# Linear attention and a gated MLP in one kernel: Tile orders the engines' queues by its detailed timing simulation instead of its simple one

## The chip, the cores and the metric

The kernel runs on one core of one Trainium2 chip. The time is the device time of one execution in microseconds (us), as the median over several runs. The core has five engines with a queue each: TensorE (PE, with its weight loads as PEld), VectorE (DVE), ScalarE (ACT), GpSimd (POOL) and SyncE (SP). SyncE's queue here issues nearly all transfers between the chip's memory and the core; ScalarE's queue issues the stores of the attention result and of the output.

## What is computed

Two stages follow one another. The first is attention with random features for 8 batches and 8 heads of 576 tokens with 64 channels, and 128 features; the second is a gated layer over the 4608 tokens of 512 channels with 1536 hidden columns.

```python
def phi(x):
    proj = np.einsum('bhsd,md->bhsm', x, omega)
    sq = np.sum(x * x, axis=-1, keepdims=True) / 2.0
    h = proj - sq
    h = h - np.max(h, axis=-1, keepdims=True)
    return np.exp(h) / np.sqrt(m)
q_p, k_p = (phi(q_s), phi(k_s))
kv = np.einsum('bhsm,bhsd->bhmd', k_p, v)
z = np.sum(k_p, axis=2)
num = np.einsum('bhsm,bhmd->bhsd', q_p, kv)
den = np.einsum('bhsm,bhm->bhs', q_p, z)[..., None] + 1e-06
attn = (num / den).astype(np.float32)

x = attn.transpose(0, 2, 1, 3).reshape(B * S, H * D)
gate = 1.0 / (1.0 + np.exp(-(x @ w_gate)))
val = x @ w_val
out = (gate * val @ w_out).astype(np.float32)
```

The weights arrive as 64-bit floats and are converted on the core.

## The kernel before

**How the numbers are kept.** A 32-bit operand of a large product is split in two parts: `split` (lines 68 to 71) writes a rounded high part with ScalarE (L70) and the remainder with VectorE or GpSimd (L71). Each product then takes three matmuls: low by high, high by low, high by high. `from_float64` (L74 to L97) turns a piece of the 64-bit weights into 32-bit floats with six VectorE instructions (L78, L81, L85, L89, L93, L95) and one addition on GpSimd (L96). The pieces are called `e` for the first eight column tiles and `c` for the 14 pieces after them; a `c` piece also gets four GpSimd subtractions (L173) and is stored to a scratch tensor `w32` in memory (L174).

**Attention** (L486 to L695). Tokens are taken two batches at a time, heads in pairs, by generators that yield between steps. `norms` loads tokens (`nat`, L492), squares them on ScalarE (L494) and sums them on VectorE (L496, L500). `projected` loads a transposed operand (`raw`, L512), splits it (`hi`, `lo`), multiplies it with omega (`pp`, L540 to L542), and takes maxima on VectorE (`mx` L545, `hm` L549). `keys` loads values (`v`, L564), takes exponentials on ScalarE (`kp`, L580), multiplies them with the values (`pkv`, L588) and copies the result (`kv`, L593). `queries` subtracts on VectorE (`sub` L606, `h` L608), transposes on TensorE (`pt`, L619), takes exponentials (`qp`, L621), multiplies with `kv` (`pn`, L631), divides on VectorE (`den` L636, `inv` L640, `x` L642), transposes back (`px`, L648), copies on ScalarE (`xs`, L654) and stores to a scratch tensor `xT` (L656). Up to six such generators are active at a time and take turns (`attention`, L674).

**The gated layer.** `first_pass` (L220) loads 512 tokens from `xT` (`load`, L217), splits them (`xe`), and for the first four hidden column tiles forms gate and value products (`gv`, L240), a tanh (L261) and a product on VectorE (L268), which is stored (`ye`, L273). Its steps are traced between attention steps, as soon as the attention result that they need has been traced. `second_pass` (L387) does the other hidden columns by a seven-product scheme for 2 x 2 blocks (`operands` L277, `gated` L326, matmuls `gw` at L344); units of weights come back from `w32` and are split (`unit`, L185). `last` (L436) loads the gated values (`yr`, L431 and L433), splits them, multiplies them with the output weights (`po`, L458), combines and stores the output.

**What sets the order in a queue.** The Python code traces instructions in one program order. When the context of Tile, the library that it is written in, closes, Tile plays the program through a simulated machine. On each engine it takes, among the instructions whose operands and buffers the simulated machine finds ready, the one that was traced first. The order in which they were taken is the order of that engine's queue on the chip, and the semaphores are set for it. Buffers of a tag (`bufs=`) are given out in the same play, so an instruction that needs a buffer waits there for its release. An instruction can be pinned behind the one traced before it on its engine:

```python
pin = tc.keep_in_program_order
...
pin(nc.scalar.activation(out=p1, in_=v0, func=AF.Copy))
```

Pinned are the second pass's matmuls, its elementwise work and its stores, the work of `operands`, and the loads of `gated_values`. Not pinned are attention, the conversions, `load`, the first pass, the first units, and in `last` everything but the loads. PSUM has eight banks: six of tag `at`, two of tag `gv`; `any_bank` takes them in turn.

## Time and profile before

| | |
|---|---|
| median of 3 runs | 1264.21 us |
| lowest and highest | 1254.57, 1267.41 us |
| the profiled execution, its own time | 1253.32 us |
| its span, first to last instruction | 1251.5 us |
| instructions | 23829 |
| chain that ended last, TensorE's share | 74% |
| moved by DMA | 219.41 MB, mean 175 GB/s |

The profiled execution's own time is its span and what lies around it. In the profile a group is named by its line and by the tiles that it writes and reads: `ppk` is the `pp` tile of keys, `ppq` that of queries, and so on. SPq and ACTq are the DMA queues of SyncE and ScalarE. "A <- B" in a table of waits means that A's engine stood idle until B was done. A TensorE that is busy is not at its peak, since matmuls are pipelined and their ends are modelled.

### The profile page before, as it was taken

The page shows a single profiled execution, that of the slowest core. Times are in us where ns is not written, and L with a number is a line of the kernel's source. Part 1 is how long each engine was busy: PE and PEld are TensorE (multiplying, and loading weights), DVE is VectorE, ACT ScalarE, POOL GpSimd, SP SyncE. Part 2 cuts the span into 40 slices and gives each one's busy share as a digit, 9 for nine tenths or more (in the row PEclk, how much of TensorE's full clock was granted, in tenths as well). Part 3 has the DMA queues.
Part 4 walks back from the last instruction along what each step waited for, and adds up shares of the span by engine and source line. Part 5 has one row for each costly group of instructions (what it writes and reads, how often), then busy time and mean ns, then how long its engine had stood idle before and what let it go on. Part 6 is the DMA issues. An engine that isn't in the chain of part 4 may idle for free.

```text
span 1251.5 us, 23829 instructions
## 1 busy us (share of the span) xinstructions
PE 1179.0 (94%) x8828; PEld 1115.9 (89%) x8828; DVE 857.7 (69%) x1799; ACT 531.4 (42%) x1160; POOL 543.9 (43%) x577
## 2 busy tenths in 40 slices
PE   6889879999998999999999999999998899999998
PEld 6789868888787988778999999999998899999998
DVE  4887797997978565542666656665658787777773
ACT  5545565565553645252423232332225343434331
POOL 2545255554766423032366666666665311111110
PEclk7687989999999999999999999999999999999999
DMA  7655767777674532172432333233337676666662
GB/s 254 218 183 178 244 228 256 262 249 257 210 255 172 180 97 84 45 247 98 173 122 90 123 123 125 106 134 123 123 117 257 198 229 198 202 187 189 191 195 93
DMA packets 102356, 219.41 MB, mean 175 GB/s; under 512 B 10848, under 2 KB 41824, under 8 KB 98144
## 3 DMA queue, kind: packets, MB, share of 16 engines
q1 hardware_dynamic: 85392, 198.94, 47.6%
q10 hardware_dynamic: 16848, 18.95, 4.3%
q8 instruction: 70, 1.15, 0.4%
q14 instruction: 46, 0.38, 0.1%
HBM read 141.82 MB, written 76.02 MB: 174 GB/s over the span
## 4 chain that ended last, share of the span: by engine, by line
PE 74%; DVE 11%; DMA 6%; issue 4%; POOL 3%; ACT 2%; SPq 1%; ACTq 0%; DVEq 0%; POOLq 0%
PE gw L344 27%; PE po L458 20%; PE gv L240 11%; PE pnq L631 4%; PE pkv L588 4%; PE ptq L619 2%; DMA natk<-kn 1%; DVE mxq L545 1%; DMA xT<-xsq 1%; PE ppk L540 1%; DVE hmq L549 1%; PE pxq L648 1%; PE ppk L541 1%; POOL xe L71 1%; PE ppk L542 1%
## 5 line engine op out<-in xcount | busy, mean ns | idle before, releaser
L344 PE MATMUL gw<-xl,u 128*128 128x256 f32 x3024 | 363.5, 283 | 3.6 <-DVE u L324 3.6
L344 PEld LDWEIGHTS gw<-xl,u 128*128 128x128 f32 x3024 | 362.5, 190 | 4.5 <-DVE u L324 4.4
L458 PE MATMUL po<-u,yh 128*128 128x256 f32 x1512 | 272.3, 283 | 0.0
L458 PEld LDWEIGHTS po<-u,yh 128*128 128x128 f32 x1512 | 234.9, 191 | 0.0
L458 PE MATMUL po<-u,yl 128*128 128x256 f32 x756 | 214.4, 284 | 3.5 <-DVE yl L71 3.5
L240 PE MATMUL gv<-xe,wh 128*128 128x512 f32 (+1 forms) x640 | 202.5, 389 | 5.2 <-POOL xe L71 5.0
L70 ACT ACTIVATE yh<-yr 128x896 fp32r<-128x896 f32 x108 | 100.1, 950 | 159.1 <-PE po L458 88.5
L458 PEld LDWEIGHTS po<-u,yl 128*128 128x128 f32 x756 | 144.5, 191 | 4.1 <-DVE yl L71 4.1
L240 PEld LDWEIGHTS gv<-xe,wh 128*128 128x128 f32 x640 | 116.3, 192 | 25.3 <-POOL xe L71 9.7
L71 POOL TENSOR_TENSOR yl<-yr,yh 128x896 fp32r<-128x896 f32 x17 | 38.0, 2238 | 215.5 <-PE po L458 126.8
L240 PE MATMUL gv<-xe,wl 128*128 128x512 f32 (+1 forms) x320 | 124.3, 390 | 5.2 <-ACT ge L261 3.0
L71 DVE TENSOR_TENSOR yl<-yr,yh 128x896 fp32r<-128x896 f32 x91 | 100.8, 1123 | 29.3 <-PE po L458 17.1
L324 DVE TENSOR_TENSOR u<-gw,p 128x256 f32<-128x256 f32 x144 | 60.7, 422 | 58.1 <-PE gw L344 49.8
L71 POOL TENSOR_TENSOR lok<-rawk,hik 128x256 fp32r<-128x256 f32 (+1 forms) x80 | 56.3, 722 | 95.9 <-ACT hik L70 92.3
L71 POOL TENSOR_TENSOR loq<-rawq,hiq 128x256 fp32r<-128x256 f32 (+1 forms) x80 | 59.9, 761 | 78.1 <-ACT hiq L70 78.0
L588 PE MATMUL pkv<-v,kpk 128*128 128x66 f32 x512 | 85.1, 292 | 9.1 <-ACT kpk L580 8.5
L588 PEld LDWEIGHTS pkv<-v,kpk 128*128 128x128 f32 x512 | 78.8, 214 | 16.4 <-ACT kpk L580 14.2
L449 DVE TENSOR_TENSOR yr<-yr 128x128 f32<-128x128 f32 x144 | 60.6, 455 | 40.9 <-DMA yr<-ye 40.5
L71 POOL TENSOR_TENSOR xe<-xr,xe 128x512 fp32r<-128x512 f32 (+1 forms) x40 | 49.9, 1264 | 87.3 <-ACT xe L70 85.9
L631 PEld LDWEIGHTS pnq<-kv,qpq 128*128 128x128 f32 (+1 forms) x640 | 70.8, 190 | 9.0 <-ACT qpq L621 5.1
L631 PE MATMUL pnq<-kv,qpq 128*128 128x66 f32 (+1 forms) x640 | 74.7, 273 | 3.6 <-ACT qpq L621 3.0
L580 ACT ACTIVATE kpk<-ppk,nb 128x128 f32<-128x128 f32 x256 | 69.6, 391 | 15.3 <-DVE nb L567 15.2
(108 smaller groups left out, 2159.5 us busy)
## 6 DMA issues: line engine op xcount, KB each, us to landing
yl<-yl SPq DMA_DIRECT2D x36, 896.0 KB, 3.8
yr<-yl SPq DMA_DIRECT2D x72, 448.0 KB, 3.8
xr<-xT SPq DMA_DIRECT2D x68, 256.0 KB, 4.4
c<-w SPq DMA_DIRECT2D x14, 1024.0 KB, 6.3
w<-c SPq DMA_DIRECT2D x14, 1024.0 KB, 4.5
v<-va SPq DMA_DIRECT2D x32, 330.0 KB, 4.0
natk<-kn SPq DMA_DIRECT2D x36, 256.0 KB, 4.7
natq<-qn SPq DMA_DIRECT2D x36, 256.0 KB, 3.9
```

The lines of the kernel that those rows point to most:

```text
L70: nc.scalar.activation(out=hi, in_=x, func=AF.Copy)
L71: (lo_engine or nc.vector).tensor_tensor(out=lo, in0=x, in1=hi.bitcast(F32), op=ALU.subtract)
L240: nc.tensor.matmul(gv, lhsT=u[:, s], rhs=v, start=(m == 0), stop=(m == 3 * KC - 1))
L324: return nc.vector.tensor_tensor(out=o, in0=a, in1=b, op=ALU.add)
L344: nc.tensor.matmul(o, lhsT=u[:, k, s], rhs=v[:, kc, :], start=(first and m == 0), stop=(m == 5), skip_group_check=not first,)
L449: nc.vector.tensor_tensor(out=raw[:, o], in0=raw[:, a], in1=raw[:, b], op=op)
L458: nc.tensor.matmul(o, lhsT=u[:, i, :], rhs=v[:, k, :], start=(j + m == 0 and n in (1, 6, 5, 4)), stop=(j == NPAIR - 1 and m == 2), skip_gr ...
L540: nc.tensor.matmul(o, lhsT=lo[:, c], rhs=omH, start=True, stop=False)
L580: nc.scalar.activation(out=kp[t][:, h, :], in_=pp[:, 2 * i + h, :], func=AF.Exp, bias=nb[:, t - t0, h : h + 1], scale=SCALE,)
L588: nc.tensor.matmul(pkv[:, h, :], lhsT=kp[b * MID + i][:, h, :], rhs=v[:, i, h, :], start=(i == 0), stop=(i == MID),)
L619: nc.tensor.transpose(out=pt[:, i, :], in_=h_sb[:, i, :], identity=id_sb)
L631: nc.tensor.matmul(pn[r, 2 * i + h, :], lhsT=qp[:, 2 * i + h, r], rhs=kvs[u, p, bb][:, h, :], start=True, stop=True,)
```

## The change

One argument of the context is set. The traced program is the same, instruction for instruction; the simulated machine that Tile plays it through is another one. The simple machine runs an engine's instructions one after another with a duration each. The detailed one models, for each engine, a sequencer and a queue of issued instructions of limited length apart from the engine itself, the travel of semaphore updates, transfers that share the DMA engines, and a TensorE clock that depends on its activity. The rule of choice (ready, then traced first) and the pins stay.

```diff
     out = nc.dram_tensor("out", (B * S, DM), F32, kind="ExternalOutput").ap()
-    with tile.TileContext(nc) as tc:
+    with tile.TileContext(nc, schedule_with_timeline_sim=True) as tc:
         attn_glu_kernel(tc, *args, out)
```

## Prediction

> **What bounds the kernel now.** I read the page's first two parts, then a table of stretches, then the waits of TensorE and of the SyncE DMA queue in the first 560 us, then two short pieces of timeline. The page first: busy time, share of the span, instructions; and the granted TensorE clock in 40 slices, in tenths.

> ```profile
> PE 1179.0 (94%) x8828; PEld 1115.9 (89%) x8828; DVE 857.7 (69%) x1799; ACT 531.4 (42%) x1160; POOL 543.9 (43%) x577
> PEclk7687989999999999999999999999999999999999
> ```

> TensorE is busy for 1179.0 of 1251.5 us, so at most 72.5 us of idle time can be won from it, and the clock is below full almost only in the first six slices (188 us). The stretches show where both losses lie (length, then busy us of PE, PEld, DVE, ACT, POOL; granted clock; DMA share; GB/s):

> ```profile
> 0.00:200.00 200.00, 162.07 (x1026) 150.88 (x1026) 148.58 (x325) 111.49 (x302) 89.83 (x99) 0.81 0.66 218
> 200.00:400.00 200.00, 184.88 (x1296) 162.15 (x1296) 176.86 (x380) 106.86 (x291) 121.76 (x125) 0.98 0.69 241
> 400.00:560.00 160.00, 152.47 (x1027) 133.05 (x1028) 93.46 (x240) 79.91 (x204) 46.76 (x56) 1.00 0.40 129
> 560.00:940.00 380.00, 379.65 (x3009) 371.42 (x3008) 216.37 (x453) 113.48 (x217) 223.69 (x261) 1.00 0.33 123
> 940.00:1000.00 60.00, 53.28 (x411) 52.05 (x410) 47.09 (x77) 25.74 (x34) 25.95 (x23) 0.94 0.70 228
> 1000.00:1251.50 251.50, 246.62 (x2067) 246.41 (x2065) 175.31 (x327) 93.94 (x113) 35.91 (x16) 1.00 0.60 185
> ```

> TensorE's idle time is 37.9 + 15.1 + 7.5 = 60.5 us before 560 (attention woven with the first GLU pass), and 0.4 + 6.7 + 4.9 = 12.0 us after it. So the first 560 us are bounded by chains between engines with TensorE close behind, and the rest by TensorE itself. In the first stage TensorE waits for these (in all, times, longest; the first four of fifteen rows, and the last):

> ```profile
> PE ptq L619 <- DVE hq L608: 13.4, 12, 2.6
> PE ppk L540 <- POOL lok L71: 9.6, 2, 8.1
> PE pkv L588 <- ACT kpk L580: 8.5, 9, 1.9
> PE gv L240 <- POOL xe L71: 5.0, 11, 1.6
> ...
> PE pnq L631 <- DVE xq L642: 0.6, 1, 0.6
> ```

> The fifteen rows sum to 59.1 us. One wait of 8.1 us is the start, before any operand has arrived, and no order removes it: 51.0 us are left. All of it is for elementwise results, none for a load directly.

> **Part 1: what the change does.** No operation is added or removed. Every tile, buffer count, transfer and matmul stays. What moves is the place of an instruction in its engine's queue, and which buffer of a tag it gets. Tile takes, on each engine, the earliest instruction of the program that its simulated machine finds ready; the change swaps the machine. So the cost of the edit is the difference between two orders, and nothing in this trace shows the second one. I bound it by stage.

> **Part 2: after 560 us, zero.** Matmuls and elementwise work of the second pass carry an explicit pin to the instruction traced before them on their engine, so they keep their order. The output stage (`last`) is not pinned, but its matmuls accumulate over six pairs in four banks, and its loads are pinned. TensorE's waits there, in two groups, are part of the 12.0 us idle. The gain is at most 12.0 us; the loss I bound by another turn of the transition at 940 to 1000, 6.7 us. I take 0: what covers the elementwise work is TensorE at 0.4 us idle in 380.

> **Part 3: the first 560 us, what order can win.** Nothing here is pinned. How far is the present order wrong for the chip? The clearest witness is SyncE's DMA queue, where a command that cannot start holds all loads behind it:

> ```profile
> SPq L273 <- DVE ye L268: 57.7, 13, 16.3
> SPq L174 <- POOL c L173: 52.2, 14, 5.9
> SPq L217 <- DMA xT<-xsq: 47.3, 12, 8.9
> SPq L512 <- POOL lok L71: 43.4, 23, 6.1
> SPq L564 <- PE pkv L588: 38.6, 12, 5.4
> SPq L512 <- POOL loq L71: 27.1, 18, 5.7
> SPq L564 <- PE pxq L648: 18.2, 4, 5.7
> SPq L273 <- DVE denq L636: 12.7, 1, 12.7
> ```

> Two kinds are mixed. The L273 and L174 rows are stores whose data did not exist yet, and L217 is a load of attention output whose store had not landed: 57.7 + 52.2 + 47.3 + 12.7 = 169.9 us in which the queue was ordered as if producers and transfers were faster than they are. The L512 and L564 rows are loads whose buffer was still read: 43.4 + 38.6 + 27.1 + 18.2 = 127.3 us, which a better order cannot give a buffer, only move out of others' way. The first kind is 169.9 / 297.2 = 57%. The compute queues err in the same manner; ACT, POOL and PE at 25 us:

> ```profile
> 25.61 0.28 ACT L593 ACTIVATE kv<-pkv 128x132 f32<-128x132 f32 x1 [2.95 <-PE pkv L588]
> 25.79 1.52 ACT L70 ACTIVATE hik<-rawk 128x256 fp32r<-128x256 f32 x5
> 26.27 4.07 POOL L71 TENSOR_TENSOR lok<-rawk,hik 128x256 fp32r<-128x256 f32 x6 [15.28 <-ACT hik L70]
> 27.05 0.58 PE L540 MATMUL ppk<-omH,lok 128*128 128x256 f32 x1 [1.48 <-POOL lok L71]
> ```

> ScalarE stood 2.95 us at a copy that waited for TensorE, with five splits of loaded keys queued behind it; TensorE then ran dry for 1.48 us for the splits. If 57% of the 51.0 us is such misordering, a machine that times things right wins at most 29 us. At the other end it wins nothing, because the later operand only takes the place of the earlier. With no row that favours either end I take the middle, 14 us.

> **Part 4: the clock.** A stall here is paid twice. DVE and TensorE around 176 us, and two stretches:

> ```profile
> 174.31 0.15 DVE L549 SCALAR_TENSOR_TENSOR hmq<-mxq,sqq 128x4 f32<-128x4 f32 x1
> 174.37 1.22 DVE L89 SCALAR_TENSOR_TENSOR c<-c 128x1024 uint32<-128x1024 uint32 x1
> 175.51 0.72 DVE L606 TENSOR_TENSOR subq<-sqq,hmq 128x4 f32<-128x4 f32 x1
> 176.26 0.69 DVE L496 TENSOR_REDUCE ssq<-x2q 128x8 f32<-128x512 f32 x1
> 176.86 0.68 DVE L608 SCALAR_TENSOR_TENSOR hq<-ppq,subq 128x512 f32<-128x512 f32 x1
> ```

> ```profile
> 177.69 1.09 PE L619 MATMUL ptq<-id_sb,hq 128*128 128x128 f32 x4 [2.59 <-DVE hq L608]
> ```

> ```profile
> 174.00:178.00 4.00, 1.41 (x12) 1.19 (x11) 3.96 (x7) 3.04 (x7) 1.41 (x2) 0.96 0.97 343
> 178.00:181.00 3.00, 3.00 (x16) 3.00 (x15) 2.57 (x4) 1.01 (x2) 0.35 (x1) 0.50 0.31 82
> ```

> After 2.59 us without a matmul the next 3 us run at 0.50. Over 0 to 200 the clock is 0.81 in 162.07 us of busy time: 162.07 x 0.19 = 31 us of lost speed as an upper end. If 14 of 51 us of stalls go, 27% of that would go with them, 8 us; at the other end none, since the dips hang on the few longest gaps. I take half, 4 us.

> [...]

> **The sum.** 0 + 14 + 4 = 18 us. The profiled execution took 1253.3 us (span 1251.5): 1235. It lies 0.9% under the median of the runs, 1264.2, which is what will be compared, so 1264.2 - 18 = 1246 us. At the good end 29 us of stalls and, with 57% of the stalls, 57% of 31 = 17.7 us of clock: 1264.2 - 46.7 = 1217.5.

> **Rivals.** *Nothing to gain (about 1264).* The waits are for buffers and for chains that have no slack, not for order. For it: the 127.3 us of buffer waits; DVE at 176.86 of 200 us in the second stretch, where any order keeps it full. [...] That the two machines give almost one order is the same case: 1264.

> *Slower (about 1290).* The same piece of timeline shows it. Between hmq and subq, 0.15 us each but for their waiting, stands a weight conversion of 1.22 us, and between subq and hq a reduction of 0.69: work that was ready filled a moment in which the chain was not. A machine with longer delays between dependent instructions finds the chain unready more often, and puts such fillers into more of the groups.

> ```profile
> L608 DVE SCALAR_TENSOR_TENSOR hq<-ppq,subq 128x512 f32<-128x512 f32 (+1 forms) x80 | 49.3, 628 | 0.2
> ```

> Now 12 of the 80 groups make TensorE wait, 13.4 us, 1.1 us each. With 24 more it is 27 us, 1264.2 + 27 = 1291. It decides against the change from about 30 more groups on if the 18 us are won elsewhere as well, and from 12 more on (13 us) if they are not. Against it: the present machine already lets fillers in, and after 400 us DVE has room (93.46 of 160).

> **How the numbers follow.** A measurement of this kernel can tell about 1% from no change, 12.6 us: under 1251.6 is faster, over 1276.8 slower. My forecast, faster through fewer misplaced commands, has 0.42, at 1246. No gain or a gain below 1% has 0.30. Slower by fillers has 0.28. The likeliest case's own range is 1217 to 1252; the range that should hold eight in ten goes from the middle of its better half, 1222, to the slower rival's price, 1290.

> **What would show it.** Part 3 is right if the L273, L174 and L217 waits of the SyncE queue fall well under 169.9 us in the first stage and TensorE's idle time before 560 us falls from 60.5 to about 46; if those waits fall and the idle time stays, the first rival holds. Part 4: the clock of the first 200 us rises from 0.81 to about 0.84. Part 2: TensorE's idle time from the start of the second pass to the end stays near 12 us. The slower rival shows as more than 12 waits of ptq for hq, each behind a conversion or reduction on DVE. The forecast is wrong if attention simply ends later because TensorE was given first-pass matmuls ahead of the short attention steps: then the stretch before 560 us is longer at equal idle time, and the dense matmuls after it are fewer.

## The result and the profile after

The changed kernel takes **1316.26 us** (median of 4 runs, 1311.83 to 1322.52) against 1259.91 us for the kernel before (4 runs beside it): a ratio of **1.0446, interval 1.0369 to 1.0524**. It is slower by 56 us; 1246 us was forecast. Times here and below are medians of all executions of a kernel, while ratios leave out slow ones, over 1.5% above the kernel's fastest: two of four of `q_group`, one of four of `t_elem`, one of ten of `t_all`.

First the page of the changed kernel: busy time, share of the span, instructions of each engine; then the granted clock in 40 slices.

```profile
PE 1191.3 (91%) x8828; PEld 1133.2 (87%) x8828; DVE 877.9 (67%) x1799; ACT 529.9 (40%) x1160; POOL 547.8 (42%) x577
PEclk7568878899999999989999999999999999999999
```

The numbers of instructions are those of before. The busy times have hardly moved, but TensorE's share fell from 94% to 91%: the same work, with more idle time in it. The chain that ended last says where it was lost. From the chain of the kernel before, in order of time (start, length, what), the start of the second pass:

```profile
611.74 329.96 PE gw L344 x2766
```

And from the chain of the changed kernel:

```profile
670.47 330.07 PE gw L344 x2766
```

The second pass starts 58.7 us later and takes as long as before: the spans, 1251.5 and 1310.0 us, differ by 58.5. So all of the loss is made before that point. The last copy of an attention result to be stored (`xs`, L654) starts at 528.6 us before and at 586.0 us after, 57.4 us later, so it is made while attention lasts. I cut the two kernels at those moments (length, then busy us of PE, PEld, DVE, ACT, POOL; granted clock; DMA share; GB/s). The kernel before:

```profile
0.00:528.60 528.60, 469.19 (x3220) 422.01 (x3221) 404.25 (x927) 282.35 (x774) 248.79 (x271) 0.92 0.59 199
528.60:1251.50 722.90, 709.79 (x5610) 693.94 (x5608) 453.41 (x872) 249.07 (x387) 295.10 (x306) 0.99 0.47 158
```

The changed kernel:

```profile
0.00:586.00 586.00, 481.02 (x3219) 438.68 (x3220) 420.65 (x927) 281.42 (x773) 251.00 (x271) 0.88 0.54 180
586.00:1310.00 724.00, 710.27 (x5610) 694.56 (x5609) 457.25 (x872) 248.48 (x387) 296.76 (x306) 0.99 0.46 158
```

The same numbers of instructions, to one, lie on each side of the cut, and the second rows are equal within 1.1 us in length. In the first rows TensorE's idle time goes from 528.6 - 469.2 = 59.4 to 586.0 - 481.0 = 105.0 us, 45.6 more, and its busy time grows by 11.8 us while the clock falls from 0.92 to 0.88. Idle time and longer busy time together are the 57.4 us.

What TensorE waits for in that stage, in the changed kernel (total us, times, longest):

```profile
PE ptq L619 <- DVE hq L608: 24.1, 14, 8.5
PE pkv L588 <- ACT kpk L580: 18.0, 10, 7.4
PE ptq L619 <- DVE hmq L549: 10.8, 3, 8.1
PE ppk L540 <- POOL lok L71: 8.5, 1, 8.5
PE pxq L648 <- DVE xq L642: 7.9, 8, 3.1
```

The waits for `hq` were 12 of 13.4 us in all and are 14 of 24.1: hardly more of them, but longer ones, up to 8.5 us. The longest is shown here in the timeline of TensorE and then of VectorE (start, length, engine, line, operation):

```profile
77.92 0.90 PE L619 MATMUL ptq<-id_sb,hq 128*128 128x128 f32 x3 [8.51 <-DVE hq L608]
```

```profile
73.30 0.15 DVE L549 SCALAR_TENSOR_TENSOR hmq<-mxq,sqq 128x4 f32<-128x4 f32 x1
73.37 0.67 DVE L496 TENSOR_REDUCE ssk<-x2k 128x8 f32<-128x512 f32 x1
73.97 1.21 DVE L89 SCALAR_TENSOR_TENSOR c<-c 128x1024 uint32<-128x1024 uint32 x1
75.10 0.15 DVE L606 TENSOR_TENSOR subq<-sqq,hmq 128x4 f32<-128x4 f32 x1
...
75.41 1.26 DVE L496 TENSOR_REDUCE ssk<-x2k 128x8 f32<-128x512 f32 x2
76.59 0.68 DVE L93 TENSOR_SCALAR c<-c 128x1024 uint32<-128x1024 uint32 x1
77.19 0.68 DVE L608 SCALAR_TENSOR_TENSOR hq<-ppq,subq 128x512 f32<-128x512 f32 x1
```

Between `hm` and `h` of a group of queries stand two conversion steps and three reductions of other work, 3.8 us, with TensorE dry. That the conversions are early here shows in their tiles (issue time min/median/max in ns, first and last start). Loads of `c` pieces in the kernel before:

```profile
L142 SPq DMA_DIRECT2D c<-w x14: 327/332/1262, 86.9 to 383.3; - x14
```

In the changed kernel:

```profile
L142 SPq DMA_DIRECT2D c<-w x14: 328/328/423, 59.5 to 251.7; - x14
```

VectorE has a wait that grew in the same stretch, too. In the kernel before and in the changed one (first 620 us):

```profile
DVE denq L636 <- PE pnq L631: 44.3, 38, 5.1
```

```profile
DVE denq L636 <- PE pnq L631: 68.4, 31, 8.0
```

Here VectorE's queue stands still for a short matmul of the attention, on average 1.2 us before and 2.2 us after. So there are two suspects, one on each side of the pair: work that fills VectorE's queue ahead of what TensorE needs, and work that fills TensorE's queue ahead of what VectorE needs. The last suspect shows in the order of TensorE's queue. Up to the last transpose back (`px`, L648), the first pass's matmuls (`gv`, L240) stand in runs of these lengths between attention matmuls:

```
                   gv matmuls   runs   mean length   matmuls in runs of 12 or more
before                 642       157       4.1               102
changed                642        75       8.6               418
```

A product `gv` is a group of 12 matmuls. The simple machine slips attention matmuls in between; the detailed one mostly lets a whole group go, or two (418 of 642 matmuls stand in runs of 12 or more).

### The profile page after: what moved, and what is told of

The parts are those of the page before. It is cut to its first block, busy times and chain, and to the rows that moved or that the text cites. A ratio compares the mean times of both kernels' runs of the same rounds, so it can differ in the third digit from the quotient of the medians.

```text
span 1310.0 us, 23809 instructions
## 1 busy us (share of the span) xinstructions
PE 1191.3 (91%) x8828; PEld 1133.2 (87%) x8828; DVE 877.9 (67%) x1799; ACT 529.9 (40%) x1160; POOL 547.8 (42%) x577
## 4 chain that ended last, share of the span: by engine, by line
PE 72%; DVE 14%; DMA 8%; ACT 2%; issue 2%; POOL 1%; SPq 1%; ACTq 0%; DVEq 0%; POOLq 0%
PE gw L344 26%; PE po L458 20%; PE gv L240 14%; PE pnq L631 3%; PE pkv L588 3%; DMA xT<-xsq 2%; PE ptq L619 2%; DVE mxq L545 2%; DMA c<-w 1%; DVE hq L608 1%; DMA e<-w 1%; DMA xr<-xT 1%; DVE hmq L549 1%; DVE ssk L496 1%; DMA natk<-kn 1%
## 5 line engine op out<-in xcount | busy, mean ns | idle before, releaser
L240 PE MATMUL gv<-xe,wh 128*128 128x512 f32 (+1 forms) x640 | 190.0, 384 | 2.7 <-POOL xe L71 2.7
L70 ACT ACTIVATE yh<-yr 128x896 fp32r<-128x896 f32 x108 | 99.4, 949 | 158.8 <-PE po L458 76.9
L240 PEld LDWEIGHTS gv<-xe,wh 128*128 128x128 f32 x640 | 119.1, 197 | 23.3 <-POOL xe L71 4.2
L240 PE MATMUL gv<-xe,wl 128*128 128x512 f32 (+1 forms) x320 | 122.1, 391 | 7.9 <-ACT xe L70 7.7
L71 POOL TENSOR_TENSOR yl<-yr,yh 128x896 fp32r<-128x896 f32 x17 | 37.2, 2186 | 218.4 <-ACT yh L70 194.8
L71 POOL TENSOR_TENSOR lok<-rawk,hik 128x256 fp32r<-128x256 f32 (+1 forms) x80 | 59.7, 760 | 135.6 <-ACT hik L70 123.1
L71 DVE TENSOR_TENSOR yl<-yr,yh 128x896 fp32r<-128x896 f32 x91 | 97.0, 1099 | 17.1 <-ACT yh L70 17.0
L588 PE MATMUL pkv<-v,kpk 128*128 128x66 f32 x512 | 84.9, 299 | 18.5 <-ACT kpk L580 18.0
L449 DVE TENSOR_TENSOR yr<-yr 128x128 f32<-128x128 f32 x144 | 65.8, 497 | 49.5 <-DMA yr<-ye 48.9
L588 PEld LDWEIGHTS pkv<-v,kpk 128*128 128x128 f32 x512 | 78.6, 219 | 22.5 <-ACT kpk L580 21.4
L71 POOL TENSOR_TENSOR loq<-rawq,hiq 128x256 fp32r<-128x256 f32 (+1 forms) x80 | 58.1, 737 | 88.7 <-ACT hiq L70 87.4
L619 PE MATMUL ptq<-id_sb,hq 128*128 128x128 f32 x288 | 51.9, 316 | 45.5 <-DVE hq L608 24.1
L71 POOL TENSOR_TENSOR xe<-xr,xe 128x512 fp32r<-128x512 f32 (+1 forms) x40 | 52.0, 1320 | 80.6 <-ACT xe L70 75.5
L619 PEld LDWEIGHTS ptq<-id_sb,hq 128*128 128x128 f32 x288 | 39.2, 166 | 53.3 <-issue 22.2
L631 PEld LDWEIGHTS pnq<-kv,qpq 128*128 128x128 f32 (+1 forms) x640 | 72.0, 194 | 12.6 <-ACT qpq L621 9.4
```

The lines of the kernel that those rows point to most:

```text
L70: nc.scalar.activation(out=hi, in_=x, func=AF.Copy)
L71: (lo_engine or nc.vector).tensor_tensor(out=lo, in0=x, in1=hi.bitcast(F32), op=ALU.subtract)
L240: nc.tensor.matmul(gv, lhsT=u[:, s], rhs=v, start=(m == 0), stop=(m == 3 * KC - 1))
L449: nc.vector.tensor_tensor(out=raw[:, o], in0=raw[:, a], in1=raw[:, b], op=op)
L588: nc.tensor.matmul(pkv[:, h, :], lhsT=kp[b * MID + i][:, h, :], rhs=v[:, i, h, :], start=(i == 0), stop=(i == MID),)
L619: nc.tensor.transpose(out=pt[:, i, :], in_=h_sb[:, i, :], identity=id_sb)
```

## The experiments

### Conversions: pinned, and cut

The first theory was that the early conversions cost all of it. Two edits were each made in both kernels. The first pins every instruction of a conversion behind the one traced before it on its engine:

```diff
-    nc.vector.tensor_scalar(out=t, in0=hi, scalar1=0x7FFFFFFF, scalar2=None, op0=ALU.bitwise_and)
+    pin(nc.vector.tensor_scalar(out=t, in0=hi, scalar1=0x7FFFFFFF, scalar2=None, op0=ALU.bitwise_and))
...
-            nc.sync.dma_start(out=w32[n], in_=f)
+            pin(nc.sync.dma_start(out=w32[n], in_=f))
```

> The changed kernel with every instruction of the weight conversions (VectorE L78 to L95, GpSimd L96 and L173, loads L142, stores L174) pinned behind what is traced before it on its engine. In VectorE's queue the 18 conversions then have 18 to 160 of the 160 maxima (L545) ahead of them, instead of 6 to 60 in the changed kernel and 13 to 115 in the kernel before. Theory A (the detailed machine lets the conversions run ahead of attention, and they take VectorE, GpSimd and the transfer queue from it): the loss goes, 1250 to 1280 us, VectorE in the first 200 us falls from 177 to about 150 us busy. Theory B (the attention steps themselves stand in a worse order): 1300 us or more.

> The kernel before with the same pins, as a control of the pins themselves. Both theories: within 20 us of 1260. Theory A: within 15 us of the run with the detailed machine and the same pins. Theory B: at least 35 us below it.

Measured: 1350.60 us in the changed kernel (1.0738 [1.0670, 1.0807]) and 1306.89 us in the kernel before (1.0385 [1.0330, 1.0441]; the kernel before took 1256.70 us here). The pins cost by themselves, 50 us in the kernel before, where at most 20 were expected. In the kernel before with pins the last piece is loaded at 585.3 us, not at 383.3:

```profile
L142 SPq DMA_DIRECT2D c<-w x14: 382/424/2497, 120.1 to 585.3; - x14
```

The conversions' tail is then left over at the end of attention. The test is spoilt for its purpose, since it made a new bound, but the two kernels are still 44 us apart with the conversions pinned in both.

The second edit cuts the conversion of the 14 `c` pieces to one VectorE operation:

```diff
-            for _ in converted(cv, NE * WE + n * 4 * Q):
-                yield
...
+            nc.sync.dma_start(out=bits, in_=w[:, i : i + 2 * WP, :])
+            yield
+            t = cv[:, : 2 * WP]
+            nc.vector.tensor_scalar(out=t, in0=bits[:, :, 1], scalar1=0x3FFFFFFF, scalar2=None, op0=ALU.bitwise_and)
...
+            nc.sync.dma_start(out=w32[n, :, :4], in_=f)
+            nc.sync.dma_start(out=w32[n, :, 4:], in_=f)
```

> The changed kernel without most of the conversion of the 14 pieces c: of its six VectorE and five GpSimd instructions one VectorE instruction is left, which makes finite numbers of the loaded words; they are stored in two halves. The output is then not the reference's. Theory A: the detailed machine loses nothing or little against the simple one with the same cut, at most 15 us. Theory B: it loses 40 us or more.

> The kernel before with the same cut. Theory A: 1240 to 1260 us, with the detailed machine's run at most 15 us above. Theory B: the detailed machine's run is 40 us or more above.

Measured: 1268.35 us in the changed kernel (1.0092 [1.0066, 1.0118]) and 1236.68 us in the kernel before (0.9826 [0.9768, 0.9884]). With these conversions cut the changed kernel is still 31.7 us slower, between the 15 us of the one theory and the 40 of the other. By this difference they account for 56 - 32 = 24 us of the loss, less than half; something else makes the rest.

### Which queue: orders transplanted

The traced programs are the same, so an order can be carried over. In the next kernels an edge that orders issue, but sets no semaphore, ties each instruction of chosen queues behind the one that precedes it in the kernel before. The other queues are free, under the detailed machine. The kernels differ in which queues `ORDER` lists (`t_first` also ties all that is left of a queue behind its last listed instruction):

```diff
+def fixed_order(tc):
...
+    for steps in json.loads(zlib.decompress(base64.b85decode(ORDER))).values():
...
+                tc.add_manual_dep(
+                    ins, behind.name,
+                    mybir.DependencyInfo(mybir.DependencyClass.NoSync, mybir.DependencyReason.DATA),
+                    reason="fixed_order",
+                )
...
     with tile.TileContext(nc, schedule_with_timeline_sim=True) as tc:
         attn_glu_kernel(tc, *args, out)
+        fixed_order(tc)
```

> The changed kernel, in which every instruction of all five queues is tied (issue order only) behind the one that precedes it in the kernel before: the five queues are those of the kernel before, and what the detailed machine still decides is which buffer of a tag a tile gets. If the loss is a matter of queue order alone: 1245 to 1270 us, no difference from the kernel before. If buffers count: above 1280.

> The changed kernel with TensorE's queue alone tied to the order of the kernel before; the detailed machine orders the other four around it. Theory P (TensorE is handed first-pass matmuls ahead of the short attention steps and runs dry later): 1255 to 1275. Theory E (the queues of the elementwise engines, with conversions ahead of attention steps): 1295 or more, little won.

> The changed kernel with the SyncE transfer queue alone tied to the order of the kernel before. Theory S (loads and stores stand in a worse order and arrive late, or let the conversions start early): 1255 to 1280. Theories P and E: 1295 or more.

> The changed kernel with the queues of VectorE, ScalarE and GpSimd tied to the order of the kernel before; TensorE's and SyncE's are ordered by the detailed machine around them. Theory E: 1255 to 1275. Theory P: 1285 or more, since TensorE is still given first-pass matmuls early. Theory S: 1285 or more.

> The changed kernel with all five queues tied to the order of the kernel before up to what had started there at 250 us (0.43 of TensorE's attention work, 10 of 18 conversions), and the detailed machine free from there on. Theory A+ (the loss is early: conversions and later units' norms ahead of attention steps): 1255 to 1270. Theory L (the detailed machine's order costs throughout, whatever it starts from): 1275 to 1300.

> The changed kernel with the queues of VectorE, ScalarE, GpSimd and SyncE tied to the order of the kernel before, TensorE's alone ordered by the detailed machine. If queues lose because they do not fit each other and the four tied ones leave TensorE little choice: 1255 to 1270. Theory P (TensorE's own order is the loss): 1285 or more.

> The changed kernel with all queues but SyncE's tied to the order of the kernel before. Theory S (the transfer queue's order, which alone was not enough to repair the rest): 1285 or more. Otherwise 1255 to 1270.

> The changed kernel with the queues of TensorE and SyncE tied to the order of the kernel before; those of VectorE, ScalarE and GpSimd are ordered by the detailed machine. Theory E (the elementwise queues' own order is the loss): 1285 or more. Otherwise 1255 to 1270.

The kernel before took 1254.37 us beside the first four and 1257.53 us beside the others. Attention's end is the start of the last `xs` copy.

| kernel | queues in the order of before | time, us | ratio to before | attention's end, us |
|---|---|---|---|---|
| t_all | all five | 1254.60 | 0.9986 [0.9953, 1.0019] | 529.3 |
| t_not_sp | all but SP | 1265.05 | 1.0045 [0.9999, 1.0090] | 537.6 |
| t_first | all five, up to what had started at 250 us | 1291.37 | 1.0282 [1.0238, 1.0327] | 574.1 |
| t_elem | DVE, ACT, POOL | 1304.34 | 1.0361 [1.0289, 1.0432] | 584.2 |
| t_not_pe | all but PE | 1307.72 | 1.0411 [1.0372, 1.0449] | 581.3 |
| t_sp | SP | 1309.54 | 1.0427 [1.0374, 1.0480] | 583.7 |
| t_pe_sp | PE and SP | 1315.25 | 1.0485 [1.0421, 1.0549] | 582.0 |
| t_pe | PE | 1319.26 | 1.0499 [1.0443, 1.0554] | 585.7 |

What follows. The loss is queue order and nothing else: with all five tied (t_all) the time is that of before, though the detailed machine's play still gives out the buffers. In the trace of `t_all` TensorE, VectorE and ScalarE run the same sequence of operations as before. The transfers' queue is nearly innocent (t_not_sp): its order is worth 0 to 11 us. The order that the detailed machine gives TensorE alone, among queues otherwise as before, costs 50 us (t_not_pe), and the order that it gives the elementwise queues alone costs 58 us (t_pe_sp): either is enough, and together they cost no more, 55 (t_sp). These orders are made around the tied queues, so they are not the changed kernel's own, only of its making. And the loss is made all along the stage: with the first 250 us put right, 34 us of it remain (t_first). In t_sp the 18 conversions come about as late in VectorE's queue as before, with 8 to 114 of the 160 maxima (L545) ahead of them against 13 to 115, and the whole loss is there: early conversions are not needed for it. Nor are long runs of `gv` matmuls: in t_pe they are those of before, 157 of 4.1, and nothing is won.

That two causes don't add up has a reason that the traces allow to measure. For the 80 groups of queries, this is the mean time from the start of the operand's split (`hi`, L70) to the end of the copy that is stored (`xs`, L654):

```
                 hi to xs, mean us      attention's end, us
before                29.8                   528.6
t_not_sp              30.4                   537.6
t_elem                32.7                   584.2
t_first               32.8                   574.1
t_pe_sp               32.8                   582.0
t_not_pe              33.1                   581.3
changed               33.7                   586.0
```

A group's latency is 13% longer and attention lasts 11% longer. 80 groups times the latency, divided by attention's end, gives 4.5 to 4.6 groups of queries in flight on average in each of the seven. With that number fixed, attention's rate is groups in flight over the latency of a group, whichever queue makes it long. This relation is a reading of the traces; no run changed the number in flight.

### TensorE: the interleave or attention's own order

The next kernels are the kernel *before*, under the simple machine, with TensorE's queue alone tied to a made order, so that the other queues can follow it. `q_after` takes the changed kernel's order. `q_order` takes its two sequences, attention's matmuls and the first pass's, but lets them alternate as in the kernel before. `q_group` takes the order of before with each `gv` group of 12 put in one row, at the place of its last matmul. `q_cap3` takes the order of before with no run over 3. Only the construction of the list differs; the edit is that above, without the argument of the context.

> The kernel before, with the simple machine, and TensorE's queue alone tied to the order of the changed kernel; all other queues are ordered by the simple machine around it. Control for the next two. TensorE's own order cost 50 us when the other queues were held at the order of before (1307.7 against 1257.5); if that was no artefact of queues that don't fit each other, this gives 1295 to 1310. If the other queues, now free to follow, take it back, 1255 to 1275.

> The same, but only the two sequences come from the changed kernel: the attention's matmuls follow each other as there, and so do the first pass's (L240), while the places that the first pass's matmuls take among the others (157 runs of 4.1 on average, not 75 of 8.6) are those of the kernel before. Theory 'interleave' (the detailed machine gives TensorE whole 12-matmul groups in a row and short attention matmuls wait behind them): 1250 to 1268. Rival 'attention's own order' (which groups of queries and keys go ahead of which): as the control, 1290 to 1310.

> The kernel before with TensorE's queue tied to its own order, except that the 12 matmuls of each first-pass product (L240) stand in one row, at the place of the last of them: 50 runs of 12.7 on average instead of 157 of 4.1, everything else in its order, other queues free under the simple machine. Theory 'interleave' as length of runs: 1285 to 1310. Rival 'attention's own order', or the interleave mattering by how early a product comes and not by how long its run is: 1250 to 1268.

> The kernel before with TensorE's queue tied to its own order, except that no more than 3 first-pass matmuls (L240) stand in a row while the attention lasts: the rest of a longer run follows between the next steps of the attention (264 runs of 2.4 on average instead of 157 of 4.1; none of 12 or more, before 102 matmuls in such). Length of runs as the cause: before 4.1 gave 1256, runs of 12.7 gave 1322, that is 7.7 us for each matmul of mean length, so 1.7 shorter is worth about 13: 1238 to 1252, and a version that beats both. If the length costs only from where the runs cover a whole step (10 or more): 1250 to 1260. If late products now hold up what waits for them, over 1265.

The kernel before took 1256.15 us beside the first three and 1258.11 us beside the last.

| kernel | runs of gv, mean length | time, us | ratio to before |
|---|---|---|---|
| q_after | 75 of 8.6 | 1330.70 | 1.0598 [1.0557, 1.0639] |
| q_order | 157 of 4.1 | 1268.11 | 1.0099 [1.0067, 1.0132] |
| q_group | 50 of 12.7 | 1321.82 | 1.0429 [1.0352, 1.0505] |
| q_cap3 | 264 of 2.4 | 1277.31 | 1.0174 [1.0125, 1.0222] |

Between the interleave and attention's own order, the interleave decides. With the changed kernel's own sequences and only the alternation of before, 62.6 of the 74.6 us that `q_after` loses are gone; and grouping alone, with every other relation in TensorE's queue as before, costs 54 us by its ratio. This holds for TensorE's order alone: `q_after` itself lies above the 1295 to 1310 us that were expected and loses more than the whole change, so that an order among queues that were not made with it is no plain share of the 56 us. A piece of TensorE's timeline in `q_after` shows what a run does:

```profile
135.58 1.92 PE L588 MATMUL pkv<-v,kpk 128*128 128x66 f32 x8
137.25 0.56 PE L240 MATMUL gv<-xe,wl 128*128 128x256 f32 x1
137.61 0.63 PE L240 MATMUL gv<-xe,wh 128*128 128x256 f32 x2
...
140.84 0.40 PE L240 MATMUL gv<-xe,wh 128*128 128x256 f32 x2
141.08 0.38 PE L619 MATMUL ptq<-id_sb,hq 128*128 128x128 f32 x2
141.40 0.46 PE L631 MATMUL pnq<-kv,qpq 128*64 128x66 f32 x8
141.78 0.39 PE L240 MATMUL gv<-xe,wl 128*128 128x256 f32 x1
```

Attention's 0.4 us steps, a transpose and the product with `kv`, stand behind 24 matmuls that take 3.8 us together. VectorE had written the transpose's `hq` at 136.7 us, and the last `qp` and `kv` written ahead of the product were there at 137.8, so nothing that the two steps read was missing. TensorE itself loses nothing there; VectorE does, as its wait for that product says, in `q_after` and then in `q_order` (first 620 us):

```profile
DVE denq L636 <- PE pnq L631: 78.9, 46, 8.0
```

```profile
DVE denq L636 <- PE pnq L631: 52.2, 38, 6.1
```

And what the other engines then deliver late makes TensorE idle later. Up to the end of attention, `q_after` and then `q_order`:

```profile
0.00:601.10 601.10, 493.87 (x3219) 448.68 (x3220) 413.04 (x927) 282.47 (x773) 253.36 (x271) 0.87 0.53 175
```

```profile
0.00:537.50 537.50, 460.37 (x3219) 414.25 (x3220) 409.93 (x927) 279.53 (x774) 253.64 (x271) 0.93 0.59 196
```

TensorE idles for 107.2 us in the one and 77.1 in the other, and its busy time differs by 33.5 us at clocks of 0.87 and 0.93. Of the 30 us more idle time, about 8 end with a result of VectorE, 10 with one of ScalarE and 11 with one of GpSimd: the delay spreads over all three. In the changed kernel it is VectorE above all, with 58.6 us of such idle time against 25.6 before.

`q_cap3` missed: runs shorter than those of before made it slower by 19 us, not faster by 13. So the cost doesn't grow with mean length throughout; in these orders runs of about 4 are better than 2.4 as well as than 8.6. The expectation's third case, late products that hold up what waits for them, would give a longer wait of `ye` for `gv` on VectorE. That wait is 41.7 us in `q_cap3` and 38.8 in the kernel before, so the case is not shown. Why `q_cap3` loses stays open. One rival is that any made order costs something: no run ties TensorE's queue to its own order of before under the simple machine. `t_all`, with all five queues tied, cost nothing, which speaks against it; and if all 19 us of `q_cap3` were such a price, 35 of the 54 us of `q_group` would still be the grouping's.

### VectorE: the same question

The next two kernels make the same exchange in VectorE's queue, with the other queues free under the simple machine.

> The kernel before with VectorE's queue alone tied to the order of the changed kernel, all others free under the simple machine. The three elementwise queues together cost the whole loss (1315.3). If VectorE's is the one that does it (conversions and norms between the attention's short steps): 1295 to 1320. If it is ScalarE's or GpSimd's: 1250 to 1270.

> As qd_after (VectorE's queue alone tied to the changed kernel's, 1377.9), but only the two sequences come from the changed kernel, the attention's steps and the rest (conversions, first-pass evictions), each in its order there; the places of the rest among the attention's steps are those of the kernel before. If it is again the interleave: 1255 to 1285. If it is the order of the attention's own steps in VectorE's queue: 1340 to 1380.

Measured: `qd_after` 1377.93 us (1.0961 [1.0928, 1.0994]) and `qd_order` 1393.01 us (1.1089 [1.1032, 1.1145]). The first lies far above its range: VectorE's order among queues that were not made with it loses 122 us, twice the whole change. The places of conversions and evictions among attention's steps are not what does it on this side: with those of the kernel before it is no better. But the two runs don't settle what does. TensorE's queue, free to follow, was again filled with long runs (90 of 7.1 and 77 of 8.3 on average), so its harm is in both. t_pe_sp, where TensorE's order is held at that of before, shows that the elementwise order costs 58 us without long runs; with conversions about as late as before (6 to 115 maxima ahead of them); which of its features costs them was not found. An exchange within VectorE's queue with all other queues held was not tried, because orders from two kernels, all of them fixed, can wait for each other in a circle.

## Why the prediction was wrong

**The step that failed is Part 3.** It took the difference between the two orders to lie between a win of 29 us and nothing, and the middle, 14 us. It measured as a loss: 45.6 us more idle time in attention, and 57.4 us with the clock of Part 4. The premise behind it, that a machine that times things right wins, did not hold here, and its lower bound of nothing left out that a new order can be worse. Nothing in the rows excluded that: the waits of the kernel before did not show that its order was the better of the two. What the runs showed in its place: TensorE's order from the detailed machine, with whole `gv` groups in a row, costs 50 us by itself (t_not_pe), and so does that of the elementwise queues, 58 us (t_pe_sp). For the second the cause within the order stays open.

**The witness was the wrong one.** Part 3 read "57% misordered" off the SyncE queue. Its two largest kinds of row rose in the changed kernel (first 620 us):

```profile
SPq L273 <- DVE ye L268: 73.4, 19, 7.5
SPq L217 <- DMA xT<-xsq: 56.9, 25, 8.8
...
SPq L512 <- POOL lok L71: 53.6, 23, 8.3
SPq L564 <- PE pkv L588: 53.2, 19, 10.2
```

L273 and L217 were 57.7 and 47.3 us at the same point of the stage (560 us, like 620 some 30 us behind the last copy of attention). L174 fell from 52.2 to 15.3 and the row for `denq` from 12.7 to 2.1, so the prediction's four rows sum to 147.7 us instead of 169.9: less waiting in these rows, and yet a longer stage. And t_not_sp shows that the order of this queue is worth 0 to 11 us either way: a wait in a transfers' queue is not a wait of the engine that bounds the stage.

**Part 1** was right (t_all: it is order alone; whether any buffer was given out otherwise was not looked at). **Part 2** was right: 0 was taken after 560 us, and the part after attention is 724.0 us against 722.9, with 13.7 us of TensorE's idle time against 13.1.

**Part 4** had the right coupling and the wrong sign with Part 3: a stall is paid twice, but the stalls grew, from 59.4 to 105.0 us. Its lower end took the dips to hang on the few longest gaps. The trace of the kernel before shows that in part: in the first 560 us, after the first matmul, six of the seven gaps of 1.80 us or more were followed within 2.1 us by a step at 0.50; the one of 2.75 us (ended at 134.60) was not, and gaps of 1.02, 1.17 and 1.60 us were. The clock of the first 200 us fell instead of rising from 0.81 to 0.84. In the changed kernel:

```profile
0.00:200.00 200.00, 140.71 (x823) 132.77 (x824) 176.84 (x310) 97.14 (x254) 119.60 (x113) 0.72 0.76 262
```

Over the stage that was 11.8 us of longer busy time, against the 4 us that were to be won. A slip in the working: the middle of the better half of 1217 to 1252 is 1226, not 1222; nothing hangs on it.

**The rivals.** "Nothing to gain" was wrong. "Slower (about 1290)" had the side, at too low a price, and part of the mechanism: fillers between `hm` and `h` are there (the piece at 73 us), and cutting the conversions takes 24 us off the loss. But it expected 24 more groups at 1.1 us, and there were 2 more waits and longer ones. It looked at one direction only, VectorE late for TensorE. The other direction, TensorE late for VectorE, was named in the prediction's last sentence, and the runs show it (q_order, q_group); its signature there was wrong. Idle time did not stay equal but went from 59.4 to 105.0 us, and the number of first-pass matmuls ahead of attention's end did not grow (642 in both). It was not how many were ahead, but how they were bunched.

## What to carry to other kernels

Where a latency-bound chain shares engines with bulk work, look at how the bulk work is bunched in each queue. Here two whole groups of `gv`, 24 matmuls, stood for 3.8 us ahead of two steps of 0.4 us (q_after). Over the stage VectorE waited 78.9 us for the product with `kv`, against 52.2 with the alternation of before (q_order), and TensorE idled 107.2 us against 77.1. Grouping alone cost 54 us (q_group). Finer was no better either: runs of 2.4 lost 19 us (q_cap3). A loss of this kind isn't read from busy shares (TensorE's went from 94% to 91%): measure the latency of one turn of the chain, before and after (29.8 and 33.7 us), multiply by the turns and divide by the turns in flight. When only a scheduler's choice changes, bound the outcome on both sides; then tie queues to the old order to see which of them matters. Tying one queue at a time won nothing back here (t_pe, t_sp), because the others alone were enough for the loss; leaving one queue or one group of queues free at a time (t_not_pe, t_not_sp, t_pe_sp) told them apart. Causes that run through the same chain did not add up: 50 us (t_not_pe) and 58 us (t_pe_sp) alone, 55 us together (t_sp).

## What the hardware showed

In `q_after` TensorE's clock fell to 0.50 in a gap of 2.91 us and came back 13 us after it:

```profile
126.07 1.22 PE L240 MATMUL gv<-xe,wh 128*128 128x256 f32 x4 [2.91 <-POOL xe L71]
```

```profile
122.00:126.00 4.00, 1.16 (x10) 0.95 (x9) 3.36 (x6) 2.35 (x9) 4.00 (x6) 0.95 0.58 207
126.00:134.00 8.00, 7.93 (x36) 7.75 (x36) 2.43 (x7) 3.96 (x13) 2.01 (x4) 0.50 0.42 117
134.00:139.00 5.00, 4.67 (x23) 4.66 (x23) 3.87 (x9) 1.70 (x4) 2.68 (x3) 0.50 0.91 321
139.00:142.00 3.00, 3.00 (x29) 2.76 (x29) 1.17 (x4) 1.29 (x3) 2.73 (x4) 0.96 0.38 140
```

For 13 us, in which TensorE was busy for 12.6, the granted clock stayed at 0.50; from 139 to 140 us it was 0.87 on average, and 1.00 after that. The pause of 0.33 us before the transpose at 134.35 is the only break that the waits name. Elsewhere it mostly came back sooner: in the first 200 us of the kernel before the clock fell to 0.50 eight times, and five of these dips lasted 3.41 us, the one at 178 us in the prediction among them; the other three lasted 13.65, 30.72 and 13.65 us.
